# A planned attention and gated-FFN block on one core: new marks for the planner, a finer account in it, and the last output rows by column halves

## The chip, the cores and the metric

The kernel runs on one core of a Trainium2 chip. The metric is device microseconds from the start to the end of the program.

## What is computed

One pre-norm transformer block on 2048 tokens of width 512, with 32 heads of 16 columns, and a gated feed-forward part of width 1792. Inputs and output are bf16.

```python
qkv = (x @ wqkv).reshape(B, S, 3, H, Dh)        # after a layer norm of x
scores = jnp.einsum("bhqd,bhkd->bhqk", q, k) * (Dh ** -0.5)
p = _softmax(scores, axis=-1)
o = jnp.einsum("bhqk,bhkd->bhqd", p, v)          # then @ wo
h = x + _A_ref(_layernorm(x, axis=-1), A_wqkv, A_wo)
# B: sigmoid(g) * u, g = y @ w_gate, u = y @ w_up, then @ w_down
h2 = h + _B_ref(_layernorm(h, axis=-1), B_w_gate, B_w_up, B_w_down)
```

## The kernel before

The program has three parts: a start of some 20 us (loading x, statistics, the first head group's keys and queries), the long loop, and a tail of some 30 us for the last 256 rows.

**Units and tiles.** Attention is cut into 2048 units. A unit is one head of a group of four, one tile of 128 keys, and 512 query columns (for the wide groups two heads of 256 columns). Three units make a tile `pss` in PSUM (three banks, two such tiles); there are 683 tiles. TensorE writes the scores (L1102). ScalarE takes the exponential of two or three of the units into `pt` (L1479). Where it takes two, VectorE makes the third out of 16-bit codes: one instruction from PSUM gives `J` (L1276), and for every four `J` three more instructions add a constant each (L1296, `code`); the sum of the four products stands for the exponential. So a unit that VectorE takes needs four products with the values instead of one (L1250, into the PSUM bank `acc`, with `Vaug`, which holds the values and a column for the softmax sums).

**What runs beside it.** Projections of values (`prep_v`, copied into `Vaug` by `v_out`, L236), keys and queries, the output projection, the second layer norm and the feed-forward part of the rows that are ready run between the scores and the products as "background" generators, each with its matmuls, its bank `pm` and its copies. GpSimd normalizes finished groups (L1154, L1160) and computes 1/sqrt of the variance of the second norm by two Newton steps (`newton_jobs`, L875 to L883), which VectorE's `apply` (L927) waits for. Weights of the feed-forward part stream through SP's queue, two buffers deep.

**What sets the order.** The order of all engines' instructions is written out when the program is built, by a planner: it keeps a time for each of PE, ACT, DVE and GpSimd (`T`), lets the engine that is earliest take a step (`pe_step`, `act_step`, `dve_step`, `gps_step`), and adds a cost for each. `MARKS` are three strings with a letter for each of the 683 tiles that bend its choices there. For ACT, `x` forbids giving a unit to VectorE, `j` lets VectorE's backlog grow, `o` prefers the first unit over the third, `l` closes a half-filled `J` later. For PE, `f` takes background work first, `p` presses for products, `r` and `R` change what rate of products is good enough, `w` and `v` change the room before the next scores, `a` and `b` change the credit of background work. For DVE, `c` runs code chains first, `s` and `e` change when a copy may go ahead of a `J`. Nothing of the planner runs on the chip; only the order of the instructions that it emits does.

A GpSimd job may have `lock`: while it runs, the planner lets no run of codes start on VectorE.

**The tail.** The last 256 rows get their output projection in `hps[0]` and `hps[1]` (128 rows by 512 columns, a PSUM bank each), are normed, go through the up projections in `gu[0..3]` (L209), tanh (L966) and `glu_out` (L950), and the down projection adds to `hps` (L1637). Then ScalarE and VectorE halve and copy the sums, and SP's and ACT's queues store them.

Of the kernel before, what the change touches and what calls it, by code (L numbers as in the profile page):

```python
# [9 lines left out]
FP32 = mybir.dt.float32  # L10
# [3 lines left out]
ALU = mybir.AluOpType  # L14
# [9 lines left out]
CODE_STEP = (55, 93, 24)  # L24
MARKS = {
    "A": (
        "......oojjjjj..xxx..o........jj..lll.j..x..jjx......jj..llollljjjjjj..o...ll"
        "l.x.xll....xj.....lxoll.jj.......xox.xx.x..jjojx.l.l.ox..o.o.l...x.....l...."
        "..o........jjj.o..l.......xx.lx..oo.............j..........oooooo....x.jo..."
        "o.o.j.......x..llxl..j........xljjxjjjjoox..l.lll.jj..o.l.lojjl......jjjlll."  # L30
        "l...o....l..ll.........xjoojjjjjj.j.lllljj........ojjo....l...l..jj........l"
        "jj.x....j.jllllxl.l.l..l.l.l..o.oooo.o....o..........x.....o.....o.j.o.....x"
        ".o.............x.oo.......j..x...x.......o..l...jj.jllo...j..jx...j..j......"
        "o..j.....jjj..................oooo.oolll.lll....jjojo........o.ooj......x..."
        "lll....x..lol.lo..ll......j.oooo..x..o...jo.x...lll.ox.ll.....xl..llxxllxx."
    ),
    "P": (
        "..r....vvv.v.....RRRRff.f.fff.vvvv.v.vvp.pppp......vva..pp.bp...r.wr.....w.w"
        "..b......ffRffr..wrrrr......w...........rrrr.vvvf.raRaa.ar.rrrrr..prrww.w.aa"
        ".av.vp....vvvvv...p..wr..p....vv....ff..........w.....vfpppv..b...RR.bbb..wv"  # L40
        "wrpp.a..vvvvavaap.b..bbbbb.bb..aaaar...fffffrf....fff.ppRRRRvvvvvwww..pf...."
        "RR.R..pr.prrr....wwRppR.abaa.vvvpp......aaaaaaRww.R...wR.fff.bbfv.r.RR...paa"
        "....f.....wwwwww...w.wwww.....r....vvr.....R...ffvf.fwRbwb.avv......p..rrrrr"
        ".rr....rvv.vvvwff......r..ffffvvv..f..b.a.RR.f.wv......pf.....ww......aa.r.."
        "RaRR.v.....vvff.f.p....fvvrr.rRaR.p..p.pp.aa.f..f.ffr.rrv.......R.......rvv."
        ".wwwwwwwpRvvvv.b..aa.....pvv.f.bbfbb...vvw....f.bbv.......wrr.r..bwp.b..pp."
    ),
    "D": (
        ".....ee.ee....c........c........c...e...........ss.......s...........s..ss.s"
        "................ee..................sss.e....ss.s........ee......ee..e..cc.."  # L50
        "...c.................ss...........e..sc.sss...........cc..........ccssss...."
        "ssssee........ec...................sss..ssscccces..c....cccc...s.ssssee.ceee"
        "eeeec.....c..ccccccc..........ce.............ee.......s.........s....ee....."
        "c.....e.ssse.....e....c.........e..e.ssss..ss..e..ss..sss.........s....ss..."
        "..............eeee.....c....ccc..........c..s.eee..e.e..............eee..ee."
        "eee..............cc..c..ss.ssc........eces....ss.sss......ceccc....c.c..ecec"
        ".ccc.s.s.e.......c..........ccc.s.ssss...sssss...................s........."
    ),
}

# [1 line left out]
def kernel(  # L62
# [551 lines left out]
            if key == "pm":  # L614
                super().__setitem__("open", False)

    st = State(**{"n": 0, "open": False, "cur": 0, "pm": None, "mark": None, "acc": None, "mode": "b", "work": "b", "ot": 0, "lock": (0.0, 0.0)})

    def dve(ns, fn, *deps):
        dq.append(Job(ns, fn, deps))  # L620
# [3 lines left out]
        aq.append(Job(ns, fn, deps))  # L624
        return aq[-1]

    def gps(ns, fn, *deps, lock=False):
        gq.append(Job(ns, fn, deps))
        gq[-1].lock = lock
        return gq[-1]  # L630

    def gps_step():
        t = T["G"]
        for job in gq:
            r = job.ready()
            if r is not None and r <= t + 60:
                gq.remove(job)
                job.place("G")
                if job.lock:
                    st["lock"] = T["G"] - job.ns, T["G"]  # L640
                return
        T["G"] = t + 40

    def unlocked(t):
        return st["lock"][1] if st["lock"][0] <= t < st["lock"][1] else t
# [17 lines left out]

    def pop_chain():
        c = next_chain()
        T["D"] = unlocked(T["D"]) + c.cost()
        _, _, f = c.ops.popleft()
        c.after.append(object())
        prior["op"] = c.after[-1]
        f()  # L670
        if not c.ops:
            chains.remove(c)
# [47 lines left out]
    def pm_new():  # L720
        return st["pm"]

    def prep_v(t):
        yield pe(2, pm_new(), WC["v"])
        ps = pm_tile()
        v_mm(ps, t, 0, 2)
        yield pe(2)
        v_mm(ps, t, 2, 4)
        st["pm"] = dve(591, lambda: v_out(ps, t), st["mark"])
        yield pe(0, st["pm"])  # L730

    kjob = {}
# [93 lines left out]
    def prep_q0(c):  # L826
        yield pe(2, pm_new(), mode="b", ns=600.0)
        ps = pm_tile()
        queries0(ps, c, 0, 2)
        yield pe(2, mode="b", ns=600.0)  # L830
        queries0(ps, c, 2, TQ)
        st["pm"] = dve(420, lambda: vscale0(ps, c), st["mark"])
        st["pm"] = dve(420, lambda: qscale0(ps, c), st["pm"])
        q0job[c] = dve(240, lambda: qsquare0(c, V), st["pm"])
        yield pe(0, st["pm"])
# [31 lines left out]
    def newton_jobs(dst, var, *deps):  # L867
        n = var.shape[1]
        v = small.tile([P, n], FP32, name="nv")
        y = small.tile([P, n], FP32, name="ny")  # L870
        t = small.tile([P, n], FP32, name="nt")
        V = nc.gpsimd

        def seed():
            V.tensor_scalar(out=v[:], in0=var, scalar1=1e-5, scalar2=None, op0=ALU.add)  # L875
            V.tensor_scalar(out=y[:].bitcast(I32), in0=v[:].bitcast(I32), scalar1=-0.5,
                            scalar2=float(0x5F3759DF), op0=ALU.mult, op1=ALU.add)

        def step(out):
            V.tensor_tensor(out=t[:], in0=y[:], in1=y[:], op=ALU.mult)  # L880
            V.tensor_tensor(out=t[:], in0=t[:], in1=v[:], op=ALU.mult)
            V.tensor_scalar(out=t[:], in0=t[:], scalar1=-0.5, scalar2=1.5, op0=ALU.mult, op1=ALU.add)
            V.tensor_tensor(out=out, in0=y[:], in1=t[:], op=ALU.mult)  # L883
        j = gps(1100, seed, *deps)
        j = gps(1050, lambda: step(y[:]), j)
        return gps(1050, lambda: step(dst), j)

    out_v = out[0].rearrange("(t p) d -> p t d", p=P)

# [310 lines left out]
    def av_left():  # L1200
        qc, g = gseq[st["cur"]]
        here = [un for un in avq if un.u[:2] == (qc, g)]
        return len(here) if not any(due[qc, g, j] for j in range(4)) else 1 << 30

    def av_ready(loose, rounds):
        per = [0] * 4
        uns = []
        for un in avq:
            if un.u[:2] == gseq[st["cur"]] and un.end + LAT <= T["P"] + loose and per[un.u[3]] < rounds:
                per[un.u[3]] += 1  # L1210
                uns.append((per[un.u[3]], un))
        return [un for _, un in sorted(uns, key=lambda v: v[0])]
# [4 lines left out]
    def av(rounds, loose=60.0):  # L1217
# [4 lines left out]
        if not uns:  # L1222
            return 0
        st["work"] = "a"
        T["P"] = max([T["P"] + switch("a")] + [un.end + LAT for un in uns]
                     + ([st["acc"].end + LAT] if st["acc"] is not None else []))
        st["acc"] = None
        qc, g = uns[0].u[:2]
# [146 lines left out]
    def pe_step():  # L1375
# [20 lines left out]
        got = [v for v in got if v and S_OUT * (st["mode"] != "a") + av_cost(v) <= room + 100]  # L1396
        pick = max(got, key=lambda v: len(v) / (100 * (st["mode"] == "s") + av_cost(v))) if got else []
        old = min((un.n for un in avq if un.held is None), default=e)
        press = e - old >= NPT - 1 or len(codes) >= CB - PRESS or len(first_codes) >= NJB or e == N
        press = press or st["cur"] < len(gseq) and lasts[gseq[st["cur"]]] < e  # L1400
        press = press or way == "p"
# [220 lines left out]
    release(len(bg) * FC)  # L1622
    for job in held:
        job.fn()
    nc.scalar.activation(out=small.tile([P, 1], FP32, name="warm")[:], in_=eps_t[:], func=ACT.Tanh)
    hT = fpool.tile([P, FC, HQ], BF16, name="hT")
    for k in range(FC // 2):
# [4 lines left out]
        for f in range(2):  # L1632
            pair_mm(u_ps, w[:, 1], f, whole)
        glu_out(hT, k, tanh_out(g_ps), u_ps)
    for i in range(HT):
        for f in range(FC):
            nc.tensor.matmul(hps[i], lhsT=hT[:, f, i * P:(i + 1) * P], rhs=wd[:, f, :],  # L1637
                             start=False, stop=(f == FC - 1), skip_group_check=True)
        ob = fwork.tile([P, D], BF16, name="ob") if i % 2 else work.tile([P, 2, QC], BF16, name="qd", bufs=2)[:, 0]
        m = HQ if i % 2 else 0  # L1640
        nc.scalar.activation(out=ob[:, m:D], in_=hps[i][:, m:D], func=ACT.Copy, scale=0.5)
        nc.scalar.dma_start(out=out_v[:, hf * HT + i, m:D], in_=ob[:, m:D])
        if m:
            nc.vector.tensor_scalar(out=ob[:, 0:m], in0=hps[i][:, 0:m], scalar1=0.5, scalar2=None, op0=ALU.mult)
            nc.sync.dma_start(out=out_v[:, hf * HT + i, 0:m], in_=ob[:, 0:m])

_INS = ['A_x', 'A_wqkv', 'A_wo', 'B_x', 'B_w_gate', 'B_w_up', 'B_w_down']
_OUTS = [((1, 2048, 512), 'bfloat16')]
# [24 lines left out]
```

## Time and profile before

| | |
|---|---|
| median of 3 runs | 787.62 us (786.22 to 853.66) |
| profiled execution | 787.43 us |
| its span, first to last instruction | 785.6 us |
| granted TensorE clock | 1.000 |
| PE / DVE / ACT / POOL busy | 754.2 / 723.1 / 753.5 / 47.3 us |
| first exp to last exp of the loop | 20.75 to 753.70 us |

In the profile a line of a group reads: source line, engine, operation, output from input, shapes, number, then busy time and the mean duration, then the idle time of the engine just before these instructions and what ended it. Durations of neighbours on ACT, DVE and PE overlap, as the engines are pipelined: the mean of an exp over two units is 1108 ns, while the next one starts 904 ns after it. A line of the timeline reads: start in us, length in us, engine, line, instruction, and in brackets the idle time before it and what ended that.

### The profile page before, as it was taken

What the parts mean: (1) busy time and instruction counts of PE and PEld (TensorE: products, weight loads), DVE (VectorE), ACT (ScalarE), POOL (GpSimd) and SP (SyncE); (2) the same over time, 40 slices, a digit from 0 to 9 for tenths busy, and PEclk for the clock granted to TensorE, in tenths of its full rate; (3) what the DMA queues carried; (4) which work ended last, traced back from release to release, by engine and by line L of the source; (5) the groups of instructions that cost most, each with busy time, mean ns of one, the idle gap of its engine ahead of it and who ended that gap; (6) DMA issues with size and microseconds to landing.
All of it is one profiled execution on the core that took longest, in us unless ns stands there. A gap on an engine that the chain in (4) does not pass through costs nothing.

```text
span 785.6 us, 34020 instructions
## 1 busy us (share of the span) xinstructions
PE 754.2 (96%) x15268; PEld 371.9 (47%) x15268; DVE 723.1 (92%) x1344; ACT 753.5 (96%) x785; POOL 47.3 (6%) x124
## 2 busy tenths in 40 slices
PE   8899999999999999999999999999999999999997
PEld 7323322444455534554455444554454355545555
DVE  6999998999999999998998999999999999998852
ACT  7999999999999999999999999999999999999962
POOL 2000000000010001000100002000000010000000
PEclk9999999999999999999999999999999999999999
DMA  6403013145012321231022401320222212322600
GB/s 199 121 2 76 2 29 68 32 100 177 15 30 71 96 62 27 60 104 36 10 63 76 126 20 44 91 83 10 61 72 83 63 37 84 97 80 73 175 25 21
DMA packets 93810, 52.99 MB, mean 67 GB/s; under 512 B 21520, under 2 KB 92576, under 8 KB 93664
## 3 DMA queue, kind: packets, MB, share of 16 engines
q1 hardware_dynamic: 92848, 50.56, 23.3%
q8 instruction: 119, 1.95, 1.0%
q10 hardware_dynamic: 816, 0.26, 0.1%
q14 instruction: 27, 0.22, 0.1%
HBM read 39.52 MB, written 2.11 MB: 53 GB/s over the span
## 4 chain that ended last, share of the span: by engine, by line
ACT 44%; PE 32%; issue 14%; DVE 8%; DMA 1%; POOL 1%; SPq 0%; ACTq 0%; DVEq 0%
ACT pt L1479 42%; PE pm L214 9%; PE acc L1250 9%; PE pss L1102 9%; DVE J L1276 3%; DVE code L1296 2%; PE gu L209 2%; ACT th L966 1%; PE hp L1637 1%; DVE hT L950 1%; DVE xs L1188 1%; DMA code<-in_A_x_dram 1%; DMA k<-kr 0%; POOL nt L880 0%; DVE Vaug L236 0%
## 5 line engine op out<-in xcount | busy, mean ns | idle before, releaser
L1479 ACT ACTIVATE pt<-pss 128x1024 bf16<-128x1024 f32 (+1 forms) x683 | 715.3, 1218 | 5.0 <-PE pss L1102 4.5
L1276 DVE TENSOR_SCALAR J<-pss 128x512 uint16<-128x512 f32 x503 | 334.0, 681 | 10.3 <-PE pss L1102 8.5
L1102 PE MATMUL pss<-QT,KT 32*128 32x256 bf16 (+1 forms) x3584 | 268.6, 288 | 20.9 <-ACT pt L1479 14.8
L1296 DVE TENSOR_SCALAR code<-J 128x2048 uint16<-128x2048 uint16 (+2 forms) x402 | 250.3, 656 | 0.7
L1250 PE MATMUL acc<-pt,Vaug 128*17 128x256 bf16 (+1 forms) x2699 | 234.3, 289 | 1.2 <-DVE Vaug L236 0.9
L1250 PE MATMUL acc<-code,Vaug 128*17 128x256 bf16 (+1 forms) x2655 | 196.0, 288 | 0.0
L1102 PEld LDWEIGHTS <-KT 32*128 32x128 bf16 x3584 | 90.1, 92 | 213.7 <-issue 117.3
L1250 PEld LDWEIGHTS <-Vaug 128*17 128x17 bf16 x6239 | 137.1, 90 | 100.6 <-issue 78.0
L1250 PE MATMUL acc<-J,Vaug 128*17 128x256 bf16 (+1 forms) x885 | 144.1, 288 | 0.2 <-DVE xs L1188 0.2
L214 PE MATMUL pm<-xT,wgu 128*32 128x256 bf16 x3136 | 115.3, 274 | 0.8 <-issue 0.3
L214 PEld LDWEIGHTS <-wgu 128*32 128x32 bf16 x3136 | 75.8, 96 | 26.0 <-issue 23.5
L214 PE MATMUL pm<-wd,hT 128*32 128x512 bf16 x728 | 53.5, 383 | 0.0
L950 DVE SCALAR_TENSOR_TENSOR hT<-th,pm 128x512 bf16<-128x512 f32 x49 | 33.5, 683 | 8.6 <-PE pm L214 8.0
L1154 POOL TENSOR_TENSOR o<-xs,rec 128x256 bf16<-128x256 f32 x23 | 16.7, 725 | 392.4 <-DVE rec L1150 392.4
L966 ACT ACTIVATE th<-pm 128x512 f32<-128x512 f32 x49 | 33.5, 684 | 0.2
L1188 DVE STREAM_TRANSPOSE xs<-acc 128x512 f32<-128x512 f32 x32 | 22.8, 713 | 10.7 <-PE acc L1250 10.4
L214 PEld LDWEIGHTS <-hT 128*32 128x32 bf16 x728 | 13.4, 95 | 18.0 <-issue 14.6
L214 PE MATMUL pm<-xT,wq_sb 128*32 128x512 bf16 x256 | 20.1, 383 | 0.0
L214 PE MATMUL pm<-xT,wk_sb 128*32 128x512 bf16 x256 | 19.2, 383 | 0.3 <-DVE kd L749 0.2
L214 PE MATMUL pm<-wv_sb,xT 128*32 128x448 bf16 x256 | 17.8, 356 | 0.0
L214 PE MATMUL pm<-wo_sb,ot 128*32 128x512 bf16 x224 | 16.7, 383 | 0.0
L1160 POOL TENSOR_TENSOR o<-xs,rec 128x256 bf16<-128x256 f32 x8 | 5.3, 660 | 184.6 <-DVE rec L1150 184.6
(153 smaller groups left out, 343.8 us busy)
## 6 DMA issues: line engine op xcount, KB each, us to landing
wgu<-in_B_w_gate_dram SPq DMA_DIRECT2D x49, 256.0 KB
wgu<-in_B_w_up_dram SPq DMA_DIRECT2D x49, 256.0 KB
KT<-half_neg SPq DMA_DIRECT2D x7, 512.0 KB
QT<-qd SPq DMA_DIRECT2D x28, 128.0 KB
KT<-kd SPq DMA_DIRECT2D x7, 256.0 KB
wd<-in_B_w_down_dram SPq DMA_DIRECT2D x1, 1792.0 KB
xr<-in_A_x_dram SPq DMA_DIRECT2D x14, 128.0 KB
out_dram<-ob SPq DMA_DIRECT2D x14, 128.0 KB
```

The lines of the kernel that those rows point to most:

```text
L209: nc.tensor.matmul(ps, lhsT=lhsT, rhs=rhs, start=start, stop=stop)
L214: nc.tensor.matmul(ps[r, :], lhsT=lhsT[:, r], rhs=rhs, start=start, stop=stop, tile_position=(0, 32 * j), skip_group_check=True)
L950: nc.vector.scalar_tensor_tensor(out=hT[:, 2 * k:2 * k + 2, :].rearrange("p f q -> p (f q)"), in0=th[:], scalar=1.0, in1=ps, op0=ALU.add, ...
L966: nc.scalar.activation(out=th[:], in_=ps, func=ACT.Tanh, scale=0.5)
L1102: mm = nc.tensor.matmul(pss[:, ui, a * w:(a + 1) * w], lhsT=KT[hg[a]][32 * j:32 * j + 32, kt * P:(kt + 1) * P], rhs=(QT0[q] if q < NQC and ...
L1154: V.tensor_tensor(out=o2[:, 0:NB, :].rearrange("p b (a d) -> p a b d", a=2), in0=xs[:, :, 0:DH].rearrange("p (a b) d -> p a b d", a=2), in ...
L1188: j = st["acc"] = dve(630, lambda: nc.vector.transpose(out=xs[:].rearrange("p b r -> p (b r)"), in_=acc[:]), Mark(T["P"]))
L1250: nc.tensor.matmul(acc[32 * j:32 * j + VW, a * w:(a + 1) * w], lhsT=Vaug[:, kt, 4 * hg[a] + j, :], rhs=un.ap[:, a * w:(a + 1) * w], start= ...
L1276: first = nc.vector.tensor_scalar(out=J[:, k, :], in0=src, scalar1=128 * SC * LOG2E, scalar2=float(CODE_BASE), op0=ALU.mult, op1=ALU.add)
L1296: nc.vector.tensor_scalar(out=c, in0=j, scalar1=CODE_STEP[i], scalar2=None, op0=ALU.add)
L1479: ex = nc.scalar.activation(out=pt[:, lo:lo + wa, :], in_=pss[:, lo:lo + wa, :], func=ACT.Exp, scale=SC)
L1637: nc.tensor.matmul(hps[i], lhsT=hT[:, f, i * P:(i + 1) * P], rhs=wd[:, f, :], start=False, stop=(f == FC - 1), skip_group_check=True)
```

## The change

Four edits in the planner and one in the tail.

1. The three strings of marks are replaced by others.
2. `newton_jobs` is planned as nine jobs (460 ns for the two one-input ones of the seed, then two rounds of four at 175 ns) in place of three (1100, 1050, 1050 ns). The instructions are the same ten. A GpSimd job with two inputs (`two`) that would start within the last planned code instruction of VectorE (`fast`) is put off to its end.
3. The planner remembers which job copies which values (`vland`), and does not plan a product before its values' copy has ended (`values`). When a unit has waited for three tiles and its values' copy isn't planned, the credit of background work is raised to at least 1.
4. In the tail, the sums of the right half of `hps[1]` are copied, halved, into `rest` before the up projection. The down projection of the last 128 rows is made in two column halves: the left one adds to `hps[1]`, the right one starts anew in `gu[0]`. ScalarE copies the left half; VectorE adds `rest` to the right one.

The diff, with the strings cut:

```diff
 MARKS = {
     "A": (
-        "......oojjjjj..xxx..o........jj..lll.j..x..jjx......jj..llollljjjjjj..o...ll"
...
+        "........x.oo.xoxxol....ojjoj.x.ooo....x.x....oxx..........j.jj...........o.x"
...
-    def gps(ns, fn, *deps, lock=False):
+    def gps(ns, fn, *deps, lock=False, two=True):
         gq.append(Job(ns, fn, deps))
-        gq[-1].lock = lock
+        gq[-1].lock, gq[-1].two = lock, two
...
             if r is not None and r <= t + 60:
+                if job.two and st["fast"][0] <= max(t, r) < st["fast"][1]:
+                    T["G"] = st["fast"][1]
+                    return
                 gq.remove(job)
...
     def pop_chain():
         c = next_chain()
-        T["D"] = unlocked(T["D"]) + c.cost()
+        start = unlocked(T["D"])
+        T["D"] = start + c.cost()
+        st["fast"] = start, T["D"]
...
+    vland = {("c", 0): Mark(0.0)}
...
-        st["pm"] = dve(591, lambda: v_out(ps, t), st["mark"])
+        st["pm"] = vland[t] = dve(591, lambda: v_out(ps, t), st["mark"])
...
-        st["pm"] = dve(420, lambda: vscale0(ps, c), st["mark"])
+        st["pm"] = vland["c", c] = dve(420, lambda: vscale0(ps, c), st["mark"])
...
-        j = gps(1100, seed, *deps)
-        j = gps(1050, lambda: step(y[:]), j)
-        return gps(1050, lambda: step(dst), j)
+        j = gps(460, seed, *deps, two=False)
+        for out in (y[:], dst):
+            j = gps(175, square, j)
+            j = gps(175, scaled, j)
+            j = gps(175, factor, j, two=False)
+            j = gps(175, lambda out=out: correct(out), j)
+        return j
...
+    def values(un):
+        q, g, kt, _ = un.u
+        job = vland.get(kt if max(head_groups(q, g)) else ("c", kt // TQ))
+        return 1e12 if job is None or job.end is None else job.end
+
     def av_ready(loose, rounds):
...
-            if un.u[:2] == gseq[st["cur"]] and un.end + LAT <= T["P"] + loose and per[un.u[3]] < rounds:
+            if un.u[:2] == gseq[st["cur"]] and max(un.end, values(un)) + LAT <= T["P"] + loose and per[un.u[3]] < rounds:
...
-        T["P"] = max([T["P"] + switch("a")] + [un.end + LAT for un in uns]
+        T["P"] = max([T["P"] + switch("a")] + [un.end + LAT for un in uns] + [values(un) + LAT for un in uns]
...
         old = min((un.n for un in avq if un.held is None), default=e)
+        if e - old >= 3 and any(e - un.n >= 3 and values(un) == 1e12 for un in avq):
+            credit = max(credit, 1.0)
...
     for job in held:
         job.fn()
+    rest = ptp.tile([P, GU, QC], BF16, name="pt")[:, 0, :].bitcast(FP32)
+    nc.scalar.activation(out=rest, in_=hps[1][:, HQ:D], func=ACT.Copy, scale=0.5)
...
-    for i in range(HT):
+    def leave(i, a, b, eng, src, ob, rest=None):
+        if rest is None:
+            nc.scalar.activation(out=ob[:, a:b], in_=src, func=ACT.Copy, scale=0.5)
+        else:
+            nc.vector.scalar_tensor_tensor(out=ob[:, a:b], in0=src, scalar=0.5, in1=rest,
+                                           op0=ALU.mult, op1=ALU.add)
+        eng.dma_start(out=out_v[:, hf * HT + i, a:b], in_=ob[:, a:b])
+
+    obs = [work.tile([P, 2, QC], BF16, name="qd", bufs=2)[:, 0], fwork.tile([P, D], BF16, name="ob")[:]]
+    for i, a, b, ps in ((0, 0, D, hps[0]), (1, 0, HQ, hps[1][:, 0:HQ]), (1, HQ, D, gu[0][:, 0:HQ])):
+        apart = a > 0
         for f in range(FC):
-            nc.tensor.matmul(hps[i], lhsT=hT[:, f, i * P:(i + 1) * P], rhs=wd[:, f, :],
-                             start=False, stop=(f == FC - 1), skip_group_check=True)
-        ob = fwork.tile([P, D], BF16, name="ob") if i % 2 else work.tile([P, 2, QC], BF16, name="qd", bufs=2)[:, 0]
-        m = HQ if i % 2 else 0
-        nc.scalar.activation(out=ob[:, m:D], in_=hps[i][:, m:D], func=ACT.Copy, scale=0.5)
-        nc.scalar.dma_start(out=out_v[:, hf * HT + i, m:D], in_=ob[:, m:D])
-        if m:
-            nc.vector.tensor_scalar(out=ob[:, 0:m], in0=hps[i][:, 0:m], scalar1=0.5, scalar2=None, op0=ALU.mult)
-            nc.sync.dma_start(out=out_v[:, hf * HT + i, 0:m], in_=ob[:, 0:m])
+            nc.tensor.matmul(ps, lhsT=hT[:, f, i * P:(i + 1) * P], rhs=wd[:, f, a:b],
+                             start=apart and f == 0, stop=(f == FC - 1), skip_group_check=True)
+        leave(i, a, b, nc.sync if apart else nc.scalar, ps, obs[i], rest if apart else None)
```

More of the change, by code (lines that the diff above doesn't have):

```diff
@@ L26 @@
     "A": (
-        "......oojjjjj..xxx..o........jj..lll.j..x..jjx......jj..llollljjjjjj..o...ll"
[L28 to L32, printed above, removed]
@@ L33 @@
-        ".o.............x.oo.......j..x...x.......o..l...jj.jllo...j..jx...j..j......"
-        "o..j.....jjj..................oooo.oolll.lll....jjojo........o.ooj......x..."
-        "lll....x..lol.lo..ll......j.oooo..x..o...jo.x...lll.ox.ll.....xl..llxxllxx."
+        "........x.oo.xoxxol....ojjoj.x.ooo....x.x....oxx..........j.jj...........o.x"
+        "x.o.......xx.lj.jlljjj.xox..ooxjojj.j..x.j..x..j....ooo..ooooooj.x..jjj.jj.."
+        "....jj...jjj...lol.....j..j..o....llll.jl...lll..o..............j..x..xx...."
@@ new lines @@
+        "jjjjj.jjjj.j..xxx.....j..o.....x...j.......x.ll..........................llj"
+        "jjjjj.xo...llll.......xxx..j..o.j..............j.j.x.j........x.l..........x"
+        "..............jj..xxo.j..oooo.ooo....oo......xooo....l..lllj.....x...l.....x"
+        ".....lllllll.j.l.j.......jjjjlllll....xo.....j.jjjjjj.......l..oololoooo.x.x"
+        "x..o...llll.x........o.jjjj..........l..........l.ll.lll...lllxljjl...j.jj.."
+        "...llllxl..........xxoo....jjjjj.lx....j..........j.jx.xxxxx.o.ooooo.xx...l"
@@ L36 @@
     ),
     "P": (
[L38 to L43, printed above, removed]
@@ L44 @@
-        ".rr....rvv.vvvwff......r..ffffvvv..f..b.a.RR.f.wv......pf.....ww......aa.r.."
-        "RaRR.v.....vvff.f.p....fvvrr.rRaR.p..p.pp.aa.f..f.ffr.rrv.......R.......rvv."
-        ".wwwwwwwpRvvvv.b..aa.....pvv.f.bbfbb...vvw....f.bbv.......wrr.r..bwp.b..pp."
+        "............aRR.ww........vww..p.p.pr........pp......f..ffR..a.a.aa..va..p.p"
+        "p....vvvv.vvvbb....v.vf.a.bw........................f......p.p...vvvvvv.pvbb"
+        ".b...........b.b.a...R.ppp.bR.r....b........pRRp.p..............wRRR.vvvvrr."
@@ new lines @@
+        "...rrp............f.br.v.vvvvv....pf........f....bb.....bb.bb..appp.aaa..pR."
+        "aRp.a..v.v...p............wbww.wp.f......v.vvRv.vv.R.vpv..f.ffffafpp........"
+        ".v.........RR...........RR..w...fff.ffv....p..........pvp..r..pprwrvr..brr.R"
+        "Rrr.p.........f..aaaaaa..vvv...........vv..fvvvvr....f...f.ff.rpp...R......."
+        "...............rrr...RR.ffR........brp.....ff...vvv.vvvv.w....v.wwp.....pp.p"
+        ".r.......ab..a..pppwb..p...rf...........pffrr.R......rfffv.RRf.r...w...frrr"
@@ L47 @@
     ),
     "D": (
[L49 to L54, printed above, removed]
@@ L55 @@
-        "..............eeee.....c....ccc..........c..s.eee..e.e..............eee..ee."
-        "eee..............cc..c..ss.ssc........eces....ss.sss......ceccc....c.c..ecec"
-        ".ccc.s.s.e.......c..........ccc.s.ssss...sssss...................s........."
+        "....c..................cc...ee....s..........................c..c..........."
+        ".c..sssssss..eeeeeee..e...ss..ssss..................c...c.e.ss.............."
+        "....c.s........c.eec.ssss..........ccsssss.ss...ss................e........."
@@ new lines @@
+        ".....c.ccscc.....cccsssc.ecc.c.........c.......ee...eeeee.eee..ss..........."
+        "....................e.................s.........eeee..s..............cc.scc."
+        "........c......ee.ee......c.e...c...........cc......eeee...........sc......."
+        "........es...................................c...sss.e.......c.............."
+        "c............ssssss...........eeeeees..........s..................s.c......."
+        "....s.......e.c.c.c.c.......ee....................c.....ss.sc..........c..."
@@ L615, in __setitem__ @@
                 super().__setitem__("open", False)
-    st = State(**{"n": 0, "open": False, "cur": 0, "pm": None, "mark": None, "acc": None, "mode": "b", "work": "b", "ot": 0, "lock": (0.0, 0.0)})
+    st = State(**{"n": 0, "open": False, "cur": 0, "pm": None, "mark": None, "acc": None, "mode": "b", "work": "b", "ot": 0, "lock": (0.0, 0.0), "fast": (0.0, 0.0)})
     def dve(ns, fn, *deps):
@@ L877, in seed, with square, scaled, factor @@
                             scalar2=float(0x5F3759DF), op0=ALU.mult, op1=ALU.add)
-        def step(out):
+        def square():
             V.tensor_tensor(out=t[:], in0=y[:], in1=y[:], op=ALU.mult)
+        def scaled():
             V.tensor_tensor(out=t[:], in0=t[:], in1=v[:], op=ALU.mult)
+        def factor():
             V.tensor_scalar(out=t[:], in0=t[:], scalar1=-0.5, scalar2=1.5, op0=ALU.mult, op1=ALU.add)
+        def correct(out):
             V.tensor_tensor(out=out, in0=y[:], in1=t[:], op=ALU.mult)
-        j = gps(1100, seed, *deps)
-        j = gps(1050, lambda: step(y[:]), j)
-        return gps(1050, lambda: step(dst), j)
+        j = gps(460, seed, *deps, two=False)
[5 more added lines that the diff above has]
+        return j
     out_v = out[0].rearrange("(t p) d -> p t d", p=P)
```

## The prediction

> **What bounds it now.** I read the page first: busy times, then the chain that ended last.
>
> ```profile
> span 785.6 us, 34020 instructions
> PE 754.2 (96%) x15268; PEld 371.9 (47%) x15268; DVE 723.1 (92%) x1344; ACT 753.5 (96%) x785; POOL 47.3 (6%) x124
> ACT 44%; PE 32%; issue 14%; DVE 8%; DMA 1%; POOL 1%; SPq 0%; ACTq 0%; DVEq 0%
> ```
>
> Three engines are nearly full, and the chain is mostly exponentials (L1479). The groups with shapes kept apart show how the softmax work is shared:
>
> ```profile
> L1479 ACT ACTIVATE pt<-pss 128x1024 bf16<-128x1024 f32 x504 | 492.1, 1108 | 4.5 <-PE pss L1102 4.0 <-ACT pt L1479 0.2
> L1276 DVE TENSOR_SCALAR J<-pss 128x512 uint16<-128x512 f32 x503 | 334.0, 681 | 10.3 <-PE pss L1102 8.5
> L1479 ACT ACTIVATE pt<-pss 128x1536 bf16<-128x1536 f32 x179 | 262.7, 1530 | 0.6 <-PE pss L1102 0.5
> ```
>
> There are 683 tiles of up to three units (512 columns each). In 503 of them VectorE takes one unit (a J), so ScalarE takes two. ACT's durations overlap, so I take the median distance between the starts of neighbours in the trace: 0.904 us for two units, 1.331 for three, 0.478 for a tanh. From the first exp (20.75) to the last (753.70) pass 732.9 us; 503 x 0.904 + 179 x 1.331 + 49 x 0.478 is 716.4. So ScalarE loses 16.6 us to waits in the loop, more than its idle column shows. Steps over 0.25 us late are nine, 5.8 us together; the other 10.8 us are crumbs of some 15 ns.
>
> **The change, part by part.**
>
> *The values' copies.* Around 126 to 136 us the timeline shows PE reading Vaug just behind its copy:
>
> ```profile
> 129.97 0.38 PE L1250 MATMUL acc<-pt,Vaug 128*17 128x512 bf16 x1 [0.30 <-DVE Vaug L236]
> 133.65 0.94 PE L214 MATMUL pm<-wv_sb,xT 128*32 128x448 bf16 x16
> 133.82 1.45 ACT L1479 ACTIVATE pt<-pss 128x1536 bf16<-128x1536 f32 x1 [0.45 <-PE pss L1102]
> 134.64 0.69 DVE L236 TENSOR_SCALAR Vaug<-pm,rstd 128x448 bf16<-128x448 f32 x1 [1.06 <-PE pm L214]
> 135.38 0.39 PE L1250 MATMUL acc<-pt,Vaug 128*17 128x512 bf16 x2 [0.58 <-DVE Vaug L236]
> 136.21 6.89 ACT L1479 ACTIVATE pt<-pss 128x1024 bf16<-128x1024 f32 x6 [0.93 <-PE pss L1102]
> ```
>
> The last values are projected at 133.65, copied at 134.64, and only then can PE go on; its next scores stand behind that, and ACT behind those. By start distances the two exps around it lose 0.56 and 1.05 us. After the change a product is not planned before its copy has landed (`values`), and a unit three tiles old without its values lets background work start. Copies and matmuls stay 16 and 256; prep_v is only moved. What it moves past is other background work on PE, and the norms behind it. I take 1.61 us off. Bounds: nothing (if PE is simply short there, the same work is late elsewhere), and 2.17, all that ACT loses in the 40 us from 100.75.
>
> *GpSimd.* The planner gave the seven rsqrt sequences (L875 to L883) 3 jobs with 3.2 us; now each has nine jobs of 460 and 8 x 175 ns, 100 ns apart: 2.66 us from the first start, plus waits for VectorE's code runs (L1296). Instructions stay the same 70. In the trace they take 2.7 us undisturbed (706 us), 3.4 to 3.9 in four, and 5.5 in this one:
>
> ```profile
> 472.62 2.98 POOL L880 TENSOR_TENSOR nt<-ny 128x2 f32<-128x2 f32 x1
> 472.45 3.10 DVE L1296 TENSOR_SCALAR code<-J 128x2048 uint16<-128x2048 uint16 x5
> 477.56 0.55 DVE L927 TENSOR_SCALAR xT<-h,mv,rstd 128x512 bf16<-128x512 f32 x1 [1.42 <-POOL rstd L883]
> ```
>
> A two-input op of 0.2 us sat under five code ops until they ended; the normalization L927 then stopped VectorE for 1.42 us, with J behind it, PE's scores behind that and two exps late by 0.78 and 0.40 (start distances). A plan that sees the run sets L927 later or breaks the run. I take those 1.18 us. Bounds: 2.24 (all that ACT loses from 460.75 to 500.75) and a loss, because the undisturbed budget shrinks from 3.4 (old, with its gaps) to 2.66 us: that is a rival below.
>
> The new account lets one-input GpSimd ops through. A row speaks against it:
>
> ```profile
> 628.78 0.56 POOL L875 TENSOR_SCALAR nv<-mv 128x2 f32<-128x2 f32 x1 [9.39 <-DVE mv L190]
> 629.43 0.51 POOL L876 TENSOR_SCALAR ny<-nv 128x2 int32<-128x2 int32 x1
> 628.61 1.28 DVE L1296 TENSOR_SCALAR code<-J 128x2048 uint16<-128x2048 uint16 x2
> ```
>
> Undisturbed they take 0.21 and 0.19; here both end with a code op, 0.67 us late together. The Trainium skill (SBUF — State Buffer, Who interferes with whom) states that VectorE in a 2-port mode and any GpSimd instruction lock each other out for a whole instruction, whatever its inputs. The row agrees; by the page the sum would be as in the fourth rival.
>
> *The marks.* All three strings are new: A and P agree with the old in only 281 and 209 of 683 places, D in 375, mostly dots. What decides the time is how many J there are. One unit moved to VectorE saves ACT 1.331 - 0.904 = 0.427 us and costs VectorE 0.60 for J and three quarters of a code op's 0.60 (1.29 us for two, less the overlap), 1.05 us; PE has three products more instead of one, about 0.16 us at 32 matmuls in 0.87. Marks "x", which forbid a J, go from 45 to 57; "j", which lets VectorE's backlog grow, from 81 to 89. If every further x cost a J, ACT gets 12 x 0.427 = 5.1 us. On the other side the stretches of 20 us from 20 to 740 show VectorE idle for 33 us in all (720 less 687.23), 31 units at most, 13 us of ACT. I take zero, nearest to the row (503), and keep both ends. The cover: if ACT were not what is waited for, these prices would vanish; its 716.4 of 732.9 us say it is.
>
> *The last rows.* The end of the timeline:
>
> ```profile
> 775.44 6.21 PE L1637 MATMUL hp<-wd,hT 128*128 128x512 bf16 x28
> 778.67 0.60 ACT L1641 ACTIVATE qd<-hp 128x512 bf16<-128x512 f32 x1 [3.30 <-PE hp L1637]
> 781.69 0.38 ACT L1641 ACTIVATE ob<-hp 128x256 bf16<-128x256 f32 x1 [2.42 <-PE hp L1637]
> 782.10 0.42 DVE L1644 TENSOR_SCALAR ob<-hp 128x256 bf16<-128x256 f32 x1 [5.70 <-ACT ob L1641]
> 782.56 0.33 SPq L1645 DMA_DIRECT2D out_dram<-ob  x1
> ```
>
> VectorE takes its half only after ACT has read the other half of the same bank: 0.41 us in series. Now the left half is finished first in hp1 and the right half in gu0, another bank. PE's last 14 matmuls become 28 of 256 columns: 28 x 0.1106 (12.39 us for the 112 of the up projection) = 3.10 against 14 x 0.2165 = 3.03, +0.07. The left half's reading and its DMA issue on ACT's queue (0.38 + 0.34) fall at about 780.2, beside PE; ACT's first issue ended at 779.64. VectorE then does its half (0.42, with one more input in SBUF; the 512-column form with such an input takes 683 ns against 681) and SP issues as before. Net -0.34; bounds 0 (if the transfers, not their issue, set the end) and -0.41. The added copy `rest` (0.38 us on ACT) comes at 763.14, ahead of the tanh table load. It delays the first tanh from 764.56 to 764.94, done by 765.52; its reader L950 starts at 765.84 after another VectorE op. Hidden; without that cover 0.38.
>
> **Sum** against the profiled execution, 787.43 us (span 785.6, and 1.8 around it; the median is 787.62): -0.34 - 1.61 - 1.18 = -3.13, so **784.3 us**.
>
> **Rivals.**
>
> 1. *More units for VectorE.* The new marks fill half of its 33 us: 15 more J, 6.4 us less on ACT: 784.3 - 6.4 = 777.9. For it: the idle time ahead of J and hT (10.3 and 8.6 us) ends with scores and matmuls that a better order brings sooner. Against: PE has only some 23 us left there (720 less 696.68).
>
> 2. *The other side: fewer units for VectorE.* A plan that counts more waiting sees VectorE later, and has more x. With 12 J fewer and the recovered stalls spent in other places: 787.4 - 0.3 + 5.1 = 792.2. It decides from 7 J fewer on, where 7 x 0.427 outweighs the 3 us above. Against: more "j".
>
> 3. *The stalls only move.* A new order of 683 steps has its own nine late steps; then only the tail is left: 787.1. For it: those steps are 5.8 us of 16.6, and an order tuned under one account meets the chip's waits somewhere else.
>
> 4. *rsqrt is late more often.* The budget is 2.66 us and one-input ops are let through. If each of the seven is late by that 0.67 us, and ACT loses 1.18 us for each 1.42 us of VectorE's stop, that is 7 x 0.67 x 0.83 = 3.9 us, in place of the 1.18 gained: 787.4 - 0.3 - 1.6 + 3.9 = 789.4. The same section of the Trainium skill would have it wherever a code op falls on such an op. Against: in six of seven before, L927 had other work ahead of it; only one stopped.
>
> **Chances.** Forecast 0.45, with its own range 782 to 787; rivals 0.18, 0.20, 0.10 and 0.07. The predicted time is the forecast's. The range of 8 in 10 reaches to the first and second rival, 778 to 792: about half of each lies outside. Two per cent, about what a measurement of this kernel can tell from no change, is 15.7 us. Faster by that needs more than the 31 units that VectorE's idle time allows for, or nearly so: 0.02. Slower by it needs 37 units fewer, or a stretch where the plan fails: 0.04. Within: 0.94.
>
> **What would show it.** J between 495 and 511; waits of PE and its weight loads for Vaug (now 0.9 and 2.3 us) below 1 us; no wait of L927 for GpSimd above 0.5 us; ACT's loss against its start distances 13 to 14 us in place of 16.6; VectorE's last op starting within 0.1 us of PE's end, and not after ACT. It is wrong if J moves by more than 8, which outweighs all the rest, or if late steps add up to more than before.

## The result, and the profile after

The changed kernel takes 784.8 us (median of 12 runs) against 786.85 us before (12 runs beside them); the ratio is 0.9977, interval 0.9968 to 0.9986. So it is 1.8 us faster, by the ratio, between 1.1 and 2.5 us: real, and far within 2 per cent. One of the runs before, with 853.66 us, was a slow one and is not in the ratio. The forecast was 784.3 us and a gain of 3.13. The profiled execution took 784.84 us, its span is 782.8 us, 2.8 less than before.

The page of the changed kernel, the lines that answer to those of before (busy times, chain, then the groups with shapes kept apart):

```profile
span 782.8 us, 34032 instructions
PE 756.6 (97%) x15274; PEld 374.8 (48%) x15274; DVE 720.3 (92%) x1339; ACT 755.1 (96%) x786; POOL 47.4 (6%) x124
...
ACT 42%; PE 30%; issue 13%; DVE 12%; POOL 1%; DMA 1%; SPq 0%; ACTq 0%; DVEq 0%
```

```profile
L1503 ACT ACTIVATE pt<-pss 128x1024 bf16<-128x1024 f32 x502 | 489.1, 1101 | 1.7 <-PE pss L1119 1.1
...
L1298 DVE TENSOR_SCALAR J<-pss 128x512 uint16<-128x512 f32 x501 | 332.2, 681 | 10.4 <-PE pss L1119 9.8
L1503 ACT ACTIVATE pt<-pss 128x1536 bf16<-128x1536 f32 x181 | 263.5, 1520 | 0.0
```

ScalarE does a little more (501 units went to VectorE, not 503), and waits less: 1.7 us before the two-unit exps in place of 4.5, and of those only 1.1 for scores in place of 4.0. The rest of the difference is in waits that the idle column hides, because the records of neighbours on ScalarE overlap. The distances between starts in the trace of before (0.904 us after an exp over two units, 1.331 over three, 0.478 after a tanh, when nothing is waited for) split every span of this study into four parts that add up to it:

| kernel | to the first exp | exps and tanhs back to back | lost between them | after the last exp | span |
|---|---|---|---|---|---|
| before | 20.75 | 716.38 | 16.56 | 31.92 | 785.62 |
| changed | 21.00 | 717.24 | 13.35 | 31.20 | 782.79 |

The first column moves from execution to execution: it is 20.6 to 22.3 us over the study, and 21.23 in experiment 1, which starts with the instructions of before. The change is the third column, 3.2 us less, against 0.86 more in the second for two units; the fourth gives 0.7, of which the last rows are about half (below).

Now the two places that the prediction had pointed to, in the changed kernel. First the whole list of waits that have to do with Vaug between 20 and 755 us (who waited for whom, total, times, longest):

```profile
PEld L1119 <- DVE Vaug L236: 0.4, 1, 0.4
DVE Vaug L236 <- PE pm L214: 0.2, 1, 0.2
```

No product waits for a values' copy any more; the 0.4 is a weight load of scores. Before, PE and its weight loads for the products had lost 0.9 and 2.3 us. The last copy now starts at 130.7 us, before at 134.64. Then the Newton steps near 473 us, GpSimd's line first and VectorE's below:

```profile
472.92 1.16 POOL L882 TENSOR_SCALAR nv<-mv 128x2 f32<-128x2 f32 x1 [15.69 <-DVE mv L190]
...
474.71 0.55 POOL L890 TENSOR_TENSOR nt<-nt,nv 128x2 f32<-128x2 f32 x1
```

```profile
472.75 1.27 DVE L1318 TENSOR_SCALAR code<-J 128x2048 uint16<-128x2048 uint16 x2
...
474.52 0.69 DVE L1318 TENSOR_SCALAR code<-J 128x2048 uint16<-128x2048 uint16 x1
...
477.52 0.99 DVE L944 TENSOR_SCALAR xT<-h,mv,rstd 128x512 bf16<-128x512 f32 x2
```

The run of five code operations is broken up, and L944 (L927 before) starts without a wait. GpSimd still waits twice here, once with a one-input operation (L882) under a run of two. The seven sequences take 2.7 to 5.5 us before and 3.1 to 4.4 us now: the longest is gone, but none keeps to the 2.66 us of the plan.

The end of the timeline:

```profile
773.25 4.71 PE L1673 MATMUL hp<-wd,hT 128*128 128x512 bf16 x28
...
777.80 1.69 PE L1673 MATMUL gu<-wd,hT 128*128 128x256 bf16 x14
778.00 0.38 ACT L1663 ACTIVATE ob<-hp 128x256 bf16<-128x256 f32 x1 [0.93 <-PE hp L1673]
...
779.53 0.42 DVE L1665 SCALAR_TENSOR_TENSOR ob<-gu,pt 128x256 bf16<-128x256 f32 x1 [5.32 <-PE gu L1673]
779.98 0.33 SPq L1667 DMA_DIRECT2D out_dram<-ob  x1
```

PE ends at 779.49 and VectorE starts 0.04 us later, while ACT began to read the other bank 1.5 us earlier. From the first down matmul to VectorE's end pass 6.70 us, 7.08 before.

### The profile page after: what moved, and what is told of

It reads as the page before. It is cut to its first block, busy times and chain, and to the rows that moved or that the text cites. A ratio compares the mean times of both kernels' runs of the same rounds, so it can differ in the third digit from the quotient of the medians.

```text
span 782.8 us, 34032 instructions
## 1 busy us (share of the span) xinstructions
PE 756.6 (97%) x15274; PEld 374.8 (48%) x15274; DVE 720.3 (92%) x1339; ACT 755.1 (96%) x786; POOL 47.4 (6%) x124
## 4 chain that ended last, share of the span: by engine, by line
ACT 42%; PE 30%; issue 13%; DVE 12%; POOL 1%; DMA 1%; SPq 0%; ACTq 0%; DVEq 0%
ACT pt L1503 40%; PE pm L214 10%; PE acc L1272 8%; PE pss L1119 8%; DVE J L1298 5%; DVE code L1318 4%; ACT th L983 2%; PE gu L209 2%; PE hp L1673 1%; DMA code<-in_A_x_dram 1%; DVE qd L815 0%; DVE xs L1205 0%; PE acc L209 0%; DVE ob L977 0%; DVE h L932 0%
## 5 line engine op out<-in xcount | busy, mean ns | idle before, releaser
L1318 DVE TENSOR_SCALAR code<-J 128x2048 uint16<-128x2048 uint16 (+3 forms) x399 | 249.9, 658 | 0.7
```

The lines of the kernel that those rows point to most:

```text
L1318: nc.vector.tensor_scalar(out=c, in0=j, scalar1=CODE_STEP[i], scalar2=None, op0=ALU.add)
```

## The experiments

Each time is a median; "before" is the kernel before, run beside the experiment (786.77 us for experiments 1 to 4, 786.46 for 5 to 8, 786.95 for 9 and 10). The numbers behind a ratio are its 95% interval.

**1. The last rows alone.** The diff's tail part, put on the kernel before.

> The kernel before with only the new last rows (left half first in hp1, right half in gu0); marks and account are the old ones, so all before the tail is instruction for instruction the same. Theory (VectorE's half waited for ACT's reading of the same bank): VectorE's last operation starts within 0.1 us of PE's last matmul and the time falls by 0.3 us, 786.85 to 786.5. Rival (the end is set by the transfer of the first rows, or by ACT's queue): 0, and the last DMA issue is earlier with the same end.

Measured: 786.08 us, ratio 0.9989 (0.9979 to 0.9998). VectorE's last operation starts at 781.21, 0.04 us after PE's end, and the part after the last exp is 31.61 us against 31.92: 0.31 less, as expected. From the first down matmul to VectorE's end pass 6.70 us, 0.38 less than before. The ratio's middle says 0.9 us, more than the tail has, but its interval reaches from 0.2 to 1.7 us and holds the 0.31; the times alone don't tell them apart. In the loop the profiles of the two differ although the order is the same: the exp at 159.4 us was 1.23 us late in the profile of before, where VectorE had waited 0.67 us for a DMA (`k`, at 154.46), and 0.64 us in this one, without that wait.

That the shared bank was what VectorE waited for, and not the shared output tile `ob`, the experiment does not separate. A pair in the trace of before speaks for the bank: VectorE (L1621, from 762.33) and ACT (L1619, from 762.55) write two parts of one tile `xT` at the same time, out of two banks.

**2. Values for nothing, in the order of before.**

```diff
-        nc.vector.tensor_scalar(out=Vaug[:, t, 4:H, 0:DH],
+        nc.vector.tensor_scalar(out=spare_v[:],
```

> The kernel before in the same order of instructions, but the 16 copies of the values of heads 4 to 31 go to a spare tile, and the products read constants that GpSimd writes once at the start of the loop: no product waits for a values' copy, all else is kept. Leaves out those values. Theory (PE's waits for Vaug are what makes two exps late around 134 us): ACT's loss between 126 and 140 us falls by 1.6 us and the total by as much, 786.85 to 785.2. Rival (PE is short of time there, the copies only show it): PE's idle time moves to the next thing, ACT's loss there falls by less than 0.5 us and the total stays within 0.5 us.

Measured: 784.81 us, ratio 0.9977 (0.9968 to 0.9987). ACT's part of the timeline from 120 to 142 us is one unbroken row; before it had breaks of 0.45 and 0.93 there:

```profile
119.19 23.33 ACT L1482 ACTIVATE pt<-pss 128x1024 bf16<-128x1024 f32 x21
```

In the 40 us from 80 us behind the first exp, ACT loses 0.31 us in place of 2.17. The order is the same, so it was the copies that PE, and through it ACT, waited for, and nothing else took their place. The rival falls.

**3. The factor for nothing, in the order of before.**

```diff
-                                    scalar1=mv[:, i, 0:1], scalar2=rstd[:, i:i + 1],
+                                    scalar1=mv[:, i, 0:1], scalar2=ones2[:, i:i + 1],
```

> The kernel before in the same order, but the second norm's normalization (L927) reads a constant in place of GpSimd's 1/sqrt, which is still computed: nothing waits for the Newton steps. Leaves out that factor. Theory (the one stop of 1.42 us around 476 us costs ACT 1.2 us): 786.85 to 785.7, and ACT's loss between 460 and 500 us falls from 2.2 to about 1.0 us. Rival (VectorE would next have waited for PE or a score): less than 0.4 us in all.

Measured: 786.15 us, ratio 0.9986 (0.9978 to 0.9995). The run of five is still there, but L929 (L927 before) follows without a wait:

```profile
472.97 3.09 DVE L1298 TENSOR_SCALAR code<-J 128x2048 uint16<-128x2048 uint16 x5
475.98 0.68 DVE L1278 TENSOR_SCALAR J<-pss 128x512 uint16<-128x512 f32 x1
476.58 0.53 DVE L929 TENSOR_SCALAR xT<-h,mv,ones 128x512 bf16<-128x512 f32 x1
```

ACT's loss in the 40 us from 440 us behind the first exp falls from 2.24 to 1.12 us, the expected 1.2. The medians differ by only 0.6 us, the ratio by 1.1, from 0.4 to 1.7: the time alone does not quite exclude the rival (less than 0.4), and it is ACT's loss in its place that decides.

**4. Both for nothing, in the order of the changed kernel.**

> The changed kernel in its own order with both waits taken away, values read from constants and the factor from a constant, as in the two kernels above. Theory (the new order has no stop left from either): 784.8, within 0.3 us. Rival (it has them too, only spread over small steps): 784.0 or less.

Measured: 785.39 us, ratio to before 0.9982 (0.9973 to 0.9990), the same within the interval as the changed kernel's 0.9977; the median is 0.6 us above the expectation. ACT loses 13.37 us between the exps; the changed kernel loses 13.35. Nothing of either wait is left in the new order, not in small steps either.

**5 to 8. Marks and account apart.** The changed kernel with the old marks; the kernel before (with the new last rows, like the others) with the new marks; both with all marks empty. The edits are the tables `MARKS` alone.

> The changed kernel with the marks of before: the new account alone. The order that comes out has 497 units on VectorE (503 before, 501 after). Theory (marks are worth something only under the account that they were found for; an account without its marks is no gain): by the units alone 4 x 0.427 = 1.7 us over the changed kernel, and more late steps: 790 to 800, slower than before. Rival (the account itself takes the stalls away, whatever the marks): no late step over 0.5 us at Vaug or at the Newton steps, and 786.5 or less.

> The kernel before with the new last rows and the new marks: the old account. The order has 492 units on VectorE. Theory: 9 x 0.427 = 3.8 us over the changed kernel from the units, and some late steps more: 788.6 to 793. Rival (the new marks are better in themselves, the account adds nothing): 784.8 to 786.

> The changed kernel with all marks empty; 503 units on VectorE. Theory (the loss is in ScalarE waiting, not in the share of units): over 795, with ACT's loss against its start distances 25 us or more in place of 13.4. Rival (the units set the time): 784, since 503 is two more than in the changed kernel.

> The kernel before with the new last rows and all marks empty; 501 units on VectorE. Theory: within 4 us of the new account without marks, on the slower side, because the stalls that the old account doesn't see (values' copies, runs of codes) come on top: 797 to 803. Rival (the account makes no difference without marks): within 1 us of it.

| marks, account | time, ratio to before | back to back | lost | after the last exp |
|---|---|---|---|---|
| old, new | 803.43, 1.0216 (1.0193 to 1.0239) | 718.47 | 27.39 | 34.69 |
| new, old | 796.6, 1.0126 (1.0109 to 1.0142) | 720.60 | 16.95 | 35.21 |
| none, new | 805.0, 1.0232 (1.0207 to 1.0256) | 716.38 | 30.81 | 33.64 |
| none, old | 806.79, 1.0255 (1.0235 to 1.0275) | 716.76 | 29.27 | 37.30 |

All four are slower than the kernel before, by 10 to 20 us. Neither half of the change is a gain by itself. That they are slower was expected each time, but of the four ranges only the third (over 795, loss over 25) held the time. One thing that I had not counted is the end: in these four orders background work is left over, 32 to 76 matmuls with `wgu` after the last exp where both kernels have none, and the part from the last exp to the first down matmul takes 24.1 to 27.6 us in place of 21.7. Between the third and the fourth row lie 1.8 us, and their intervals overlap: whether the account does anything without marks is not shown.

The new account with the old marks (the first row) is the sharpest of them. It does what it was made for: in the 40 us in which the copies had cost 2.17 us, ACT loses 0.53, and no row has L944 waiting for GpSimd. But the order behind that is another one, with 23 late steps over 0.25 us, 16.9 us together. The two largest, 2.3 and 2.8 us, are behind scores whose queries had not landed:

```profile
L1119 PE MATMUL pss<-QT,KT 32*128 32x256 bf16 x3072 | 204.7, 273 | 21.2 <-ACT pt L1503 11.8 <-DMA QT<-qd 5.6 <-DVE J L1298 1.5
```

Not all of that is the order: within 2 us of the end of each of these two waits TensorE's granted clock fell to 0.50 (figures in the last section), and four late steps in and just behind the slow stretches make 3.0 of the 16.9 us.

One more fact on the account: with the new marks, the part on the values (`vland`, `values` and the raised credit) changes no instruction. The program built without it is the same. The edit can have acted only through the choice of the marks; it is the order, not the rule, that has no wait for Vaug. It follows that the second row of the table differs from the changed kernel in GpSimd's account alone, and that this is worth some 12 us under these marks.

**9 and 10. More marks.** The search for marks carried on from the new ones, under the account of the change, and under one in which GpSimd's one-input operations wait for runs of codes as well:

```diff
-        j = gps(460, seed, *deps, two=False)
+        j = gps(460, seed, *deps)
...
-            j = gps(175, factor, j, two=False)
+            j = gps(175, factor, j)
```

> The changed kernel with the search for marks carried on from its own, under its own account, now up to the end of the last group and not only of the last exp: 504 units on VectorE in place of 501. Theory (what this account counts is what the chip does): 3 x 0.427 = 1.3 us from the units and about 0.9 us of waits, 782.6, with no stop at Vaug and ACT's loss about 12.5 us. Rival (the account is fitted past what it knows, such as one-input GpSimd operations): the loss grows by what the units bring, 784 to 786.

> The changed kernel with one more thing in the account: GpSimd operations of one input, too, wait for a run of codes (the two cases of two=False are taken out), and marks searched for it from the changed kernel's own; 501 units on VectorE, as many as in the changed kernel. Theory (the exemption is wrong on the chip, but its price is small): 783 to 784.5, no wait of L927 for GpSimd over 0.3 us. Rival (the exemption costs as much as in the prediction's fourth rival, up to 3.9 us): 782 or less.

Measured: 784.14 us, ratio 0.9967 (0.9957 to 0.9978) for the first, and 785.48 us, 0.9978 (0.9969 to 0.9987) for the second; the changed kernel's ratio is 0.9977. The first is the lowest median of the study, but its interval overlaps that of the changed kernel. Its profile gains by the units (715.96 back to back in place of 717.24), and its loss of 14.12 us is not the 12.5 that the theory gave; 0.72 of it is one step behind a half clock at the start (below). The second has no wait of L944 for GpSimd at all, and is no faster; the expected 783 to 784.5 was missed by a microsecond. Its marks are other ones too, so it shows only that no gain came of ending the exemption of one-input operations, not its exact cost.

## Why the prediction was right

**The values' copies**: predicted 1.61, measured in the same 40 us 2.17 - 0.55 = 1.62, and experiment 2 shows the cause. The chain PE, copy, product, scores, exp was read rightly. What took the wait away was not the rule `values`, though, which changes nothing in this order, but the marks that were found with it.

**GpSimd**: predicted 1.18; in its 40 us the loss fell by 2.24 - 0.79 = 1.45, of which experiment 3 gives 1.12 to the stop itself.

**The marks**: predicted 0 with the number of units as what decides; it moved by two, 0.86 us against the kernel. Of the twelve units that as many further x could have cost, two came. This term, put at nothing, is the one that was wrong; it is far smaller than its bounds. With it the working gives a gain of 2.27 us in place of 3.13.

**The last rows**: predicted 0.34; 6.70 in place of 7.08 us in the changed kernel, 0.38, and 0.31 in experiment 1. The part after the last exp is shorter by 0.72 in all: 0.38 here, 0.08 between the last exp and the first down matmul, and 0.26 after VectorE's end (2.84 in place of 3.09 us). The last is not the change's: it is 2.80 us in experiment 2, with the last rows of before, and 3.16 in experiment 1, with the new ones. `rest` is hidden as worked out: it runs from 760.84 to 761.23, the first tanh ends at 763.22 and its reader starts at 763.65, behind VectorE's other operation.

Sum by the four columns: +0.25 + 0.86 - 3.21 - 0.72 = -2.82. That is near the predicted 3.13 in part by luck: the loss of 16.56 us holds the 1.23 us of the exp at 159.4 us, which other executions of the same order show at 0.55 to 0.71. In the medians, where that is averaged, the change is 2.0, and by the ratio 1.8, with 3.13 outside its interval and 2.27 inside. That the time itself came within 0.5 us of the forecast is luck too: the forecast started from one execution of 787.43 us, and the median of the kernel before is 786.85.

**Rivals.** The first (more units) is false: two fewer came. The third (the stalls only move) is false: late steps over 0.25 us went from 9 with 5.75 us to 7 with 2.01, while the crumbs grew only from 10.8 to 11.3. The second (fewer units) came in miniature, 2 of its 12. The fourth (one-input operations) happened and cost little: L882 took 1.13 and 1.16 us under runs of two code operations, against 0.21 undisturbed. That a one-input operation is held at all is what the Trainium skill's rule says (SBUF — State Buffer, Who interferes with whom); the rule has the wait last for one instruction, and here it lasted over two. But L944 had other work ahead of it and waited 0.6 us in all, 0.4 at most. Experiment 10, which brought no gain, agrees. That rival had the mechanism right and the cover wrong in its price of 3.9 us.

What the prediction did not see is how much the marks are worth under either account: 20 us between none and the fitted ones, ten times the change. It read the two edits of the account as two gains to add; experiments 5 to 8 show that account and marks are one thing, an order found with an account, and that the new account with the old marks costs 17 us.

## What to carry to other kernels

Where an engine's records overlap, take the distances between starts, not the idle column: here ACT lost 16.6 us in the kernel before where the column showed some 5. A wait can be priced without touching the order, by giving the waiting instruction data that is already there; both prices found so agree with the trace to 0.3 us. The better account in this planner was worth nothing until the marks were searched anew with it, and a further search under it was expected to give 782.6 us and gave 784.1: the account's own sum is not yet the chip's time.

## What the runs showed of the hardware

A GpSimd operation that meets a run of VectorE's code operations can be held to the end of the run, not only of the operation under way: it took 2.98 us under five (472.62 in the profile of before), 1.13 and 1.16 us under two (213.53 and 472.92 in that of the changed kernel). It is not always so: at 628.78 us of the kernel before one got through between two.

In some executions TensorE's granted clock was 0.50 for 3.4 us right at the start of the loop, as in the profile of experiment 3 (columns: stretch, its length, busy time and number on PE, PEld, DVE, ACT and POOL, granted clock, DMA share, GB/s):

```profile
21.00:24.00 3.00, 3.00 (x24) 1.82 (x22) 1.95 (x5) 2.17 (x3) 0.00 (x0) 0.50 0.84 217
```

One of the first exps is late there by 0.7 to 1.0 us (experiments 2, 3, 9 and 10); the profiles of the kernel before and of the changed one have neither. It is of the size of the effects here, so single profiles of this kernel are not to be compared to less than a microsecond by their spans.

In three of the four orders of experiments 5 to 8 it also fell inside the loop, each time near the end of a wait of PE for queries:

| experiment | PE waited | wait ended at | clock 0.50 from | for |
|---|---|---|---|---|
| 5 | 2.56 us | 158.14 | 159.85 | 3.4 us |
| 5 | 2.47 us | 183.81 | 183.74 | 6.8 us |
| 7 | 2.26 us | 161.27 | 162.89 | 3.4 us |
| 8 | 2.25 us | 161.77 | 162.96 | 3.4 us |

A second wait of 1.36 us, near 187 us in experiments 7 and 8, had no such stretch behind it. Whether the wait is the cause was not tested.
